# Attention and mixer on one core: k's column maximum sent to all partitions through memory, or by a product with a diagonal

## The chip, the core and the metric

The kernel runs on one core of a Trainium2 chip. The metric is the device time of one execution in microseconds (us). TensorE is called PE here, its weight loads PEld, VectorE DVE, ScalarE ACT, GpSimd POOL and SyncE SP; SP issues the loads. Each engine executes its own instructions in order and waits on semaphores for the others.

## The reference

For 8 batches of 8 heads with 576 positions and 64 channels (all float32), a linear attention is computed and fed to a mixer:

```python
q_s = softmax(q, axis=-1)          # over the 64 channels
k_s = softmax(k, axis=2)           # over the 576 positions
kv  = einsum('bhsd,bhse->bhde', k_s, v)
x   = einsum('bhsd,bhde->bhse', q_s, kv)   # as (batch, 576, 512)
u   = x + w_tok2' relu(w_tok1' x)          # along the positions
out = u + relu(u w_ch1) w_ch2              # along the 512 channels, 1536 hidden
```

The softmax of k subtracts the maximum over all positions for each channel. The mixer's products are held to float32 accuracy by splitting each operand into a high and a low part and adding three products.

## The kernel before, in words

**Units.** A unit is one pair of heads of one batch: 128 channels by 576 positions, padded to 640. There are 32, counted n = 0 to 31. `load_unit` (L106) loads for each unit kt (k with channels on partitions), q, k (positions on partitions; only from unit 8 on) and v. The buffers are few: kt has one, q and k two each, v a ring of two.

**Softmax of k.** `softmax_k` (L179) reduces kt over positions to the maximum mc, one number for each of 128 partitions (L182, DVE). Units 0 to 7 (`on_pe`) take the exponent on kt and turn it with PE. Units 8 to 31 have k with positions on partitions already, so the 128 maxima are wanted along the free axis, on all partitions. The kernel before makes a diagonal matrix dg out of mc (L197, ACT), multiplies a matrix of ones with it on PE (L199), copies the result from PSUM to mb (L201, ACT), subtracts mb from k (L202, POOL) and takes the exponent (L203, ACT).

**The stages of a unit.** After the softmax of q (L211 to L222; its high and low parts are qh, made by ACT, and ql, made by POOL in L89), a unit has four stages: s1 turns q with DVE copies (L262, L270) and multiplies k with v (L229); s2 is the first token product (L281); s3 and s4 are h1 (L289), its split hh and hl (L295, L296), and u (L322), written to the tiles uh and ul (L328, L329).

**The groups.** The positions of all batches are cut into 9 groups of 512. For each group the channel mixer runs 12 steps f: `ch1` (12 matmuls, L341; then h2h by ACT in L343 and h2l by DVE in L344) and, one step later, `ch2` (12 matmuls, L352) into four accumulators ps_o, which `out_end` adds to the residual (L360 by POOL, L367 by DVE) and writes. Units 0 to 3 are computed ahead; in the loop over groups the four units of the next batch are spread between the steps, three steps apart. In the first group the weights are still being loaded and converted on DVE (L143 to L150).

**What sets the order.** The code is written in the order of the loops, but a scheduler, which goes by modelled times, places the instructions of each engine when the program is built (`schedule_with_timeline_sim=True`). So a changed line can move others, and each engine's row of instructions is fixed before the run. One SP queue carries all loads in its row's order; a load that waits for a buffer holds up those behind it.

Of the kernel before, what the change touches and what calls it, by code (L numbers as in the profile page):

```python
# [8 lines left out]
F32 = mybir.dt.float32  # L9
F32R = mybir.dt.float32r  # L10
U32 = mybir.dt.uint32
AF = mybir.ActivationFunctionType
# [3 lines left out]
P = 128  # L16
# [4 lines left out]
def attn_mixer_kernel(ctx: ExitStack, tc: tile.TileContext, q, k, kt, v, wt, out, dims):  # L21
# [3 lines left out]
    nc = tc.nc  # L25
# [14 lines left out]
    const = ctx.enter_context(tc.tile_pool(name="const", bufs=1))  # L40
    ld = ctx.enter_context(tc.tile_pool(name="ld", bufs=2))
    wk = ctx.enter_context(tc.tile_pool(name="wk", bufs=1))
    sm = ctx.enter_context(tc.tile_pool(name="sm", bufs=2))
    stg = ctx.enter_context(tc.tile_pool(name="stg", bufs=2))
    cv = ctx.enter_context(tc.tile_pool(name="cv", bufs=2))
    upool = ctx.enter_context(tc.tile_pool(name="upool", bufs=3))
    hpool = ctx.enter_context(tc.tile_pool(name="hpool", bufs=2))
    ps_o = ctx.enter_context(tc.tile_pool(name="ps_o", bufs=NJ, space=bass.MemoryType.PSUM))
    ps_h = ctx.enter_context(tc.tile_pool(name="ps_h", bufs=4, space=bass.MemoryType.PSUM))

    ident = const.tile([P, P], F32R, name="ident")
# [5 lines left out]
    for t in v_ring:  # L57
        nc.gpsimd.memset(t[:, :, P : P + 1], 1.0)
        nc.gpsimd.memset(t[TL:P, C, :], 0.0)

    ones = const.tile([P, P], F32, name="ones")
    nc.gpsimd.memset(ones, 1.0)


    ebias = const.tile([P, 1], F32, name="ebias")
# [17 lines left out]
    def f32(ap):  # L83
        return ap.bitcast(F32)
# [8 lines left out]
    def ps_unit(dtype=F32):  # L93

        pools = unit_banks[0]
        pool, name = pools[turn[0] % len(pools)]
        turn[0] += 1
        return pool.tile([P, 512], dtype, name=name)
# [80 lines left out]
    def softmax_k(u):  # L179
        ktt = u["kt"]  # L180
        mc = sm.tile([P, 1], F32, name="mc")
        nc.vector.tensor_reduce(mc, ktt, axis=AX.X, op=ALU.max)  # L182
        kx = u["k"]
        if u["on_pe"]:
            nc.vector.tensor_scalar(mc, mc, -1.0, None, op0=ALU.mult)
            nc.scalar.activation(ktt, ktt, AF.Exp, bias=mc)
            t = ps_unit()
            for c in range(C):
                nc.tensor.transpose(t[:, c * P : (c + 1) * P], ktt[:, c * P : (c + 1) * P], f32(ident))
            nc.scalar.copy(kx[:, 0:C, :], t.rearrange("p (c d) -> p c d", c=C))  # L190
            t = ps_unit()
            nc.tensor.transpose(t[:, 0:P], ktt[:, S0 : S0 + P], f32(ident))
            nc.scalar.copy(kx[:, C, :], t[:, 0:P])  # L193
            return

        dg = sm.tile([P, P], F32, name="dg", bufs=1)
        nc.scalar.activation(dg, f32(ident), AF.Copy, scale=mc)  # L197
        t = ps_unit()
        nc.tensor.matmul(t[:, 0:P], ones, dg, start=True, stop=True)  # L199
        mb = sm.tile([P, P], F32, name="mb", bufs=1)  # L200
        nc.scalar.copy(mb, t[:, 0:P])  # L201
        nc.gpsimd.tensor_tensor(kx, kx, mb.unsqueeze(1).broadcast_to([P, C1, P]), op=ALU.subtract)  # L202
        nc.scalar.activation(kx, kx, AF.Exp)  # L203

# [172 lines left out]
    def soft(n):  # L377
        if n < NU:
            softmax_k(units[n])
            softmax_q(units[n])  # L380
# [164 lines left out]
```

## Time and profile before

| | |
|---|---|
| median of 3 runs | 860.49 us (858.84 to 860.98) |
| the profiled execution | 860.69 us, of it 858.6 us span |
| PE, PEld busy | 814.3, 695.5 us |
| DVE, ACT, POOL busy | 494.7, 335.6, 124.4 us |
| moved by DMA | 63.5 MB |

Durations, waits and starts come from the profiled execution alone. Its span is the time from the first to the last instruction; 2.1 us of the execution's own time lie around it. Matmuls are pipelined, so a matmul's listed duration is longer than the time by which it moves the next one on.

### The profile page before, as it was taken

To read this page: it belongs to the slowest core of one execution; us is meant where nothing else is said; L and a number is where in the kernel's file an instruction comes from. 1 tells how busy PE (TensorE), PEld (TensorE's weight loads), DVE (VectorE), ACT (ScalarE), POOL (GpSimd) and SP (SyncE) were. 2 spreads that over 40 slices of the span, in tenths; PEclk is the share of its full clock that TensorE was granted. 3 is DMA by queue.
4 is the path that set the end of the run, shared out by engine and by line. 5 is a ranking of instruction groups with operands and counts; after the bars stand their busy time and mean duration, and the time that the engine had idled before them with its cause. 6 is when DMAs were issued, how large, how long until landed. Compare 5 with 4: busy or idle time off the path is not lost.

```text
span 858.6 us, 11201 instructions
## 1 busy us (share of the span) xinstructions
PE 814.3 (95%) x4224; PEld 695.5 (81%) x4224; DVE 494.7 (58%) x1093; ACT 335.6 (39%) x785; POOL 124.4 (14%) x98
## 2 busy tenths in 40 slices
PE   3668999998999999999999999999999999999997
PEld 2567787877888888888888888888888888888886
DVE  7999998966555755485557555765556332112112
ACT  5676664534434444344444443444434331111100
POOL 0000000422011411041113111311132102001100
PEclk9689999999999999999999999999999999999999
DMA  8435444331112311131122112321121001001001
GB/s 285 133 100 179 146 129 162 94 109 60 60 60 71 99 47 55 37 108 61 60 59 98 59 60 60 110 61 60 45 94 45 1 1 50 1 0 50 1 1 49
DMA packets 41685, 63.50 MB, mean 74 GB/s; under 512 B 3488, under 2 KB 22048, under 8 KB 41632
## 3 DMA queue, kind: packets, MB, share of 16 engines
q1 hardware_dynamic: 36448, 53.36, 19.8%
q10 hardware_dynamic: 5184, 9.44, 2.9%
q8 instruction: 33, 0.54, 0.3%
q14 instruction: 20, 0.16, 0.1%
HBM read 53.35 MB, written 9.44 MB: 73 GB/s over the span
## 4 chain that ended last, share of the span: by engine, by line
PE 79%; DVE 13%; DMA 4%; issue 1%; ACT 1%; POOL 1%; SPq 0%; DVEq 0%; POOLq 0%; ACTq 0%
PE ps_h L341 31%; PE ps_o L352 31%; PE ps_h L322 7%; PE ps_h L281 5%; PE ps_h L229 3%; DMA stg<-in_w 2%; DVE cv_s L145 1%; PE ps_h L289 1%; DVE stg L148 1%; DVE cv_s L150 1%; DVE q_t L270 1%; DMA q_t<-in_q 1%; DVE stg L146 1%; DVE cv_s L143 1%; DVE q_t L212 1%
## 5 line engine op out<-in xcount | busy, mean ns | idle before, releaser
L344 DVE SCALAR_TENSOR_TENSOR h2l<-ps_h,h2h 128x512 fp32r<-128x512 f32 x108 | 74.2, 687 | 182.9 <-ACT h2h L343 182.9
L341 PE MATMUL ps_h<-uh,c1h 128*128 128x512 f32 x432 | 172.6, 400 | 0.9 <-ACT k_t L193 0.7
L341 PE MATMUL ps_h<-ul,c1h 128*128 128x512 f32 x432 | 171.7, 397 | 0.4 <-DVE ul L329 0.4
L341 PE MATMUL ps_h<-uh,c1l 128*128 128x512 f32 x432 | 171.4, 397 | 0.0
L352 PE MATMUL ps_o<-h2h,c2l 128*128 128x512 f32 x432 | 169.0, 391 | 0.0
L343 ACT ACTIVATE h2h<-ps_h 128x512 fp32r<-128x512 f32 x108 | 64.4, 597 | 261.1 <-PE ps_h L341 250.5
L352 PE MATMUL ps_o<-h2h,c2h 128*128 128x512 f32 x432 | 165.1, 393 | 1.5 <-DVE stg L367 1.5
L352 PE MATMUL ps_o<-h2l,c2h 128*128 128x512 f32 x432 | 157.3, 396 | 0.0
L270 DVE COPY q_t<-cv_s 32x160 f32<-32x160 f32 (+1 forms) x264 | 73.3, 278 | 69.9 <-POOL ql L89 66.7
L202 POOL TENSOR_TENSOR k_t<-k_t,mb 128x640 f32<-128x640 f32 x24 | 37.7, 1572 | 459.7 <-ACT mb L201 307.6
L341 PEld LDWEIGHTS ps_h<-ul,c1h 128*128 128x128 f32 x432 | 82.0, 190 | 19.8 <-DVE ul L329 0.6
L341 PEld LDWEIGHTS ps_h<-uh,c1h 128*128 128x128 f32 x432 | 82.2, 190 | 17.5 <-ACT k_t L193 0.9
L352 PEld LDWEIGHTS ps_o<-h2h,c2h 128*128 128x128 f32 x432 | 80.7, 188 | 18.6 <-DVE stg L367 2.6
L341 PEld LDWEIGHTS ps_h<-uh,c1l 128*128 128x128 f32 x432 | 82.2, 190 | 16.5
L352 PEld LDWEIGHTS ps_o<-h2h,c2l 128*128 128x128 f32 x432 | 81.1, 188 | 16.1
L352 PEld LDWEIGHTS ps_o<-h2l,c2h 128*128 128x128 f32 x432 | 79.5, 188 | 15.7
L360 POOL TENSOR_TENSOR stg<-uh,ul 128x512 f32<-128x512 f32 x36 | 47.5, 1343 | 128.4 <-DMA out<-stg 76.6
L211 DVE TENSOR_REDUCE st<-q_t 128x10 f32<-128x640 f32 x32 | 26.2, 819 | 43.8 <-DMA q_t<-in_q 43.8
L89 POOL TENSOR_TENSOR ql<-q_t,qh 128x640 fp32r<-128x640 f32 x24 | 37.9, 1581 | 83.7 <-ACT qh L88 64.1
L229 PEld LDWEIGHTS ps_h<-v_ring,k_t 128*128 128x128 f32 x320 | 44.5, 203 | 4.7 <-ACT qtl L253 2.0
L229 PE MATMUL ps_h<-v_ring,k_t 128*128 128x129 f32 x320 | 46.0, 289 | 1.4 <-ACT qtl L253 1.4
L213 ACT ACTIVATE q_t<-q_t 128x640 f32<-128x640 f32 x32 | 23.7, 740 | 49.7 <-DVE q_t L212 49.7
(136 smaller groups left out, 1223.3 us busy)
## 6 DMA issues: line engine op xcount, KB each, us to landing
stg<-in_w SPq DMA_DIRECT2D x28, 512.0 KB, 3.8
kt_t<-in_kt SPq DMA_DIRECT2D x32, 320.0 KB, 3.2
q_t<-in_q SPq DMA_DIRECT2D x32, 320.0 KB, 2.9
out<-stg ACTq DMA_DIRECT2D x36, 256.0 KB, 2.2
v_ring<-in_v SPq DMA_DIRECT2D x32, 256.0 KB, 2.9
k_t<-in_k SPq DMA_DIRECT2D x24, 320.0 KB, 3.4
v_ring<-in_v SPq DMA_DIRECT2D x32, 32.0 KB, 3.1
stg<-in_w SPq DMA_DIRECT2D x1, 256.0 KB, 6.2
```

What stands on the lines that cost most here:

```text
L89: lo_eng.tensor_tensor(lo, src, f32(hi), op=ALU.subtract)
L202: nc.gpsimd.tensor_tensor(kx, kx, mb.unsqueeze(1).broadcast_to([P, C1, P]), op=ALU.subtract)
L211: nc.vector.tensor_reduce(st[:, 0, :], qt, axis=AX.X, op=ALU.max)
L229: nc.tensor.matmul(kv[:, 0 : P + 1], kx[:, c, :], vt[:, c, 0 : P + 1], start=(c == 0), stop=(c == C))
L270: eng(qx[ys, 0:n, xs], turned[xs, 0:n, ys])
L281: nc.tensor.matmul(y[:, 0:TOK], a, w, start=(i == 0), stop=(i == len(mm) - 1))
L322: nc.tensor.matmul(t[:, 0:N], a, w, start=(i == 0), stop=(i == len(mm) - 1))
L341: nc.tensor.matmul(t, a[:, n, fs], w, start=(i == 0), stop=(i == 3 * NJ - 1))
L343: nc.scalar.activation(hh, t, AF.Relu)
L344: nc.vector.scalar_tensor_tensor(hl, t, 0.0, f32(hh), op0=ALU.max, op1=ALU.subtract)
L352: nc.tensor.matmul(o, a[:, cs], w, start=(f == 0 and i == 0), stop=(f == NF - 1 and i == 2))
L360: nc.gpsimd.tensor_tensor(res[n // 2][:, n % 2, :], f32(uh), f32(ul), op=ALU.add)
```

## The change

For units 8 to 31 the maxima go through memory. One transfer writes mc, a number from each partition, to 512 B of DRAM (`row`); a second reads them back 128 times, so that each partition gets all 128 numbers (mb). The diagonal, the matrix of ones, the product, its PSUM tile and the copy are gone. Subtraction and exponent stay. Both transfers are issued by SP, on the queue of the loads.

```diff
+    dram = ctx.enter_context(tc.tile_pool(name="dram", bufs=2, space=bass.MemoryType.DRAM))
...
-    ones = const.tile([P, P], F32, name="ones")
-    nc.gpsimd.memset(ones, 1.0)
...
-        dg = sm.tile([P, P], F32, name="dg", bufs=1)
-        nc.scalar.activation(dg, f32(ident), AF.Copy, scale=mc)
-        t = ps_unit()
-        nc.tensor.matmul(t[:, 0:P], ones, dg, start=True, stop=True)
+        row = dram.tile([P], F32, name="row")
+        nc.sync.dma_start(row.rearrange("(p x) -> p x", x=1), mc)
         mb = sm.tile([P, P], F32, name="mb", bufs=1)
-        nc.scalar.copy(mb, t[:, 0:P])
+        nc.sync.dma_start(mb, row.unsqueeze(0).broadcast_to([P, P]))
         nc.gpsimd.tensor_tensor(kx, kx, mb.unsqueeze(1).broadcast_to([P, C1, P]), op=ALU.subtract)
         nc.scalar.activation(kx, kx, AF.Exp)
```

The scheduler places much else differently. Lines behind the change have other numbers in the new kernel: the kt, q, k and v loads are L110, L113, L117 and L120 to L121 (L112, L115, L119, L122 to L123 before), the reduction L180 (L182), the subtraction L198 (L202), the copies L266 (L270), h2l L340 (L344), hl L292 (L296), ql L87 (L89). L195 is the row, L197 mb. The number behind a tile's name tells its instance.

SP's loads around units 10 to 13 before; kt_t_2515 and kt_t_2734 are those of units 13 and 14, q_t_2107 is that of unit 11 and q_t_2312 that of unit 12:

```order
L112 DMA kt_t_2515<-in_kt 128x640
L115 DMA q_t_2107<-in_q 128x640
L122 DMA v_ring1_93<-in_v 128x4x128
L119 DMA k_t_2109<-in_k 128x640
L123 DMA v_ring1_93<-in_v 64x128
L112 DMA kt_t_2734<-in_kt 128x640
L115 DMA q_t_2312<-in_q 128x640
```

SP's loads at the same place now, from kt of unit 17 on; mb_2273 is that of unit 11, the rows are those of units 17 to 20, q_t_2101 is q of unit 11:

```order
L110 DMA kt_t_3331<-in_kt 128x640
L197 DMA mb_2273<-row_2271 128x128
L195 DMA row_3507<-mc_3505 128x1
L110 DMA kt_t_3546<-in_kt 128x640
L195 DMA row_3722<-mc_3720 128x1
L110 DMA kt_t_3753<-in_kt 128x640
L195 DMA row_3923<-mc_3921 128x1
L110 DMA kt_t_3954<-in_kt 128x640
L113 DMA q_t_2101<-in_q 128x640
L195 DMA row_4124<-mc_4122 128x1
```

Before, one kt load stood between the loads of two units, two units ahead; now several pairs of row and kt stand there, nine units ahead of q, and between a row and its mb stand the rows of five further units.

DVE around hl of unit 10 before; q_t_2107 is q of unit 11, which is being turned:

```order
L270 COPY q_t_2107<-cv_s_2445 32x5x32 x6
L270 COPY q_t_2107<-cv_s_2445 32x4x32 x5
L296 SCALAR_TENSOR_TENSOR hl_2368<-ps_h_2364,hh_2367 128x256
```

DVE at the same place now; the reductions are those of units 28 to 31:

```order
L180 TENSOR_REDUCE mc_5784<-kt_t_5614 128x1
L340 SCALAR_TENSOR_TENSOR h2l_2311<-ps_h_2312,h2h_2310 128x512
L180 TENSOR_REDUCE mc_5993<-kt_t_5817 128x1
L266 COPY q_t_2101<-cv_s_2437 32x5x32 x6
L266 COPY q_t_2101<-cv_s_2437 32x4x32 x5
L180 TENSOR_REDUCE mc_6210<-kt_t_6034 128x1
L292 SCALAR_TENSOR_TENSOR hl_2360<-ps_h_2356,hh_2359 128x256
L180 TENSOR_REDUCE mc_6413<-kt_t_6243 128x1
```

Reductions of units 28 to 31 now stand between the copies, h2l and hl of unit 10 and 11; the last of all 32 is the one behind hl.

POOL around units 11 and 12 before (k_t_2109 and q_t_2107 are of unit 11, k_t_2314 of unit 12):

```order
L202 TENSOR_TENSOR k_t_2109<-k_t_2109,mb_2281 128x640
L89 TENSOR_TENSOR ql_2294<-q_t_2107,qh_2293 128x640
L202 TENSOR_TENSOR k_t_2314<-k_t_2314,mb_2486 128x640
```

POOL at the same place now (ql_2083 is of unit 10, k_t_2306 of unit 12, q_t_2101 of unit 11):

```order
L87 TENSOR_TENSOR ql_2083<-q_t_1892,qh_2082 128x640
L198 TENSOR_TENSOR k_t_2306<-k_t_2306,mb_2476 128x640
L87 TENSOR_TENSOR ql_2286<-q_t_2101,qh_2285 128x640
```

The subtraction of unit 12 stood behind ql of unit 11 and stands ahead of it now.

## The prediction

> **What bounds the kernel now.** The page's table of engines comes first, then the busy time of each engine in stretches of the span.
>
> ```profile
> PE 814.3 (95%) x4224; PEld 695.5 (81%) x4224; DVE 494.7 (58%) x1093; ACT 335.6 (39%) x785; POOL 124.4 (14%) x98
> ```
> ```profile
> 150.00:175.00 25.00, 24.41 (x132) 21.09 (x132) 24.36 (x46) 12.68 (x31) 9.28 (x6) 1.00 0.27 83
> 175.00:200.00 25.00, 21.35 (x109) 17.47 (x108) 17.11 (x33) 8.92 (x23) 8.13 (x6) 0.99 0.28 94
> 200.00:225.00 25.00, 25.00 (x127) 21.33 (x126) 13.05 (x33) 9.69 (x24) 3.14 (x2) 0.94 0.17 53
> 600.00:680.00 80.00, 80.00 (x432) 69.24 (x431) 42.77 (x102) 32.01 (x81) 15.97 (x11) 1.00 0.15 50
> ```
>
> The columns after a stretch's length are PE, PEld, DVE, ACT, POOL, then the granted clock. From 200 us on PE never rests and DVE is about half idle. From 150 to 175 us DVE is as full as PE, and from 175 to 200 us PE loses 3.65 us. The product that the change removes (L199) first runs at 153.9 us, so nearly all of it lies where PE sets the time.
>
> How much of PE's time one product takes is read from the chain of waits, which follows PE there. A unit is one pair of heads of one batch; units 8 to 31 use this path, 24 in all, and the product for unit n stands right behind L229 of unit n-1.
>
> ```profile
> 153.88 0.22 PE ps_h L199 x2
> ...
> 250.97 0.22 PE ps_h L199 x2
> ...
> 677.69 0.22 PE ps_h L199 x2
> ```
> ```profile
> L199 PE MATMUL ps_h<-dg,ones x48: 272/274/275, 153.7 to 677.6; 128*128 128x128 f32 x48
> ```
>
> The first, the fifth and the last of the 24 are shown: each moves the chain on by 0.22 us, although its two passes are listed with 274 ns each, because matmuls overlap. The 0.22 is the price; 24 times two times 0.274 (13.2 us) would count the overlap.
>
> **The change, part by part.** What it removes from PE is 24 x 0.22 = 5.3 us, four of them (units 8 to 11) before 245 us and 20 (4.4 us) after it. From ACT it removes two operations for each unit:
>
> ```profile
> L197 ACT ACTIVATE dg<-ident,mc x24: 402/405/417, 136.8 to 656.0; 128x128 f32<-128x128 f32 x24
> L201 ACT COPY mb<-ps_h x24: 245/248/265, 154.2 to 677.9; 128x128 f32<-128x128 f32 x24
> ```
>
> That is 24 x (0.405 + 0.248) = 15.7 us of an engine that is busy 39%; PE's work covers it, so I count nothing.
>
> What it adds are 48 small transfers on SP's queue, a write of 512 B (row) and a read of 64 KB (mb) for each unit. How long such a pair takes is bounded by the nearest transfers: the output, which goes to memory, and v's tail, which is read.
>
> ```profile
> out<-stg ACTq DMA_DIRECT2D x36, 256.0 KB, 2.2
> v_ring<-in_v SPq DMA_DIRECT2D x32, 32.0 KB, 3.1
> ```
>
> 2.2 + 3.1 = 5.3 us from maximum to subtraction. Only units 8 and 9 can feel this. For unit 8 the reduction and the next q load stand so:
>
> ```profile
> 135.33 0.81 DVE L182 TENSOR_REDUCE mc<-kt_t 128x1 f32<-128x640 f32 x1
> ```
> ```profile
> 140.64 0.33 SPq L115 DMA_DIRECT2D q_t<-in_q  x1
> ```
>
> The row lands at 135.33 + 0.81 + 0.33 + 2.2 = 138.7 us, so SP, which waits for it before it issues mb, is free again 1.9 us before q of unit 9 goes out anyway. If that cover were gone, it would cost its 2.2 us twice at most.
>
> From unit 10 on the rows run far ahead, and here lies what the order does besides. The reduction's result no longer waits for an ACT operation and a PE product of its own unit, so kt loads and reductions of units 10 to 31 are pulled forward: in the new order the last reduction stands just behind L296 of unit 10, while the old order has one in each unit. These are linked. There is one kt buffer: the load of unit n+1 waits for the reduction of unit n, and on SP it stands behind the row of unit n. DVE executes in order, so a reduction whose kt has not landed holds up everything behind it. One link costs:
>
> ```profile
> L112 SPq DMA_DIRECT2D kt_t<-in_kt x32: 327/333/549, 0.7 to 590.2; - x32
> ...
> DMA to landing us min/median/max: 2.8/3.2/6.6
> ```
> ```profile
> L182 DVE TENSOR_REDUCE mc<-kt_t x32: 799/809/829, 4.0 to 611.8; 128x1 f32<-128x640 f32 x32
> ```
>
> The reduction is 0.81, the row's issue (as that of kt) 0.33, and kt's landing 2.8 to 3.2: 3.95 to 4.35 us, plus what the row's own packets cost the kt load that follows them in the same queue. I take 4.3: the landing at 3.15, since k, v and q loads still fall among these.
>
> What is available? The relevant rows of DVE and PE:
>
> ```profile
> 186.45 1.25 DVE L367 TENSOR_TENSOR stg<-ps_o,stg 128x512 f32<-128x512 f32 x2
> ...
> 193.01 4.80 DVE L270 COPY q_t<-cv_s 32x160 f32<-32x160 f32 x11 [4.72 <-POOL ql L89]
> 197.84 0.43 DVE L296 SCALAR_TENSOR_TENSOR hl<-ps_h,hh 128x256 fp32r<-128x256 f32 x1
> ```
> ```profile
> 241.42 0.42 DVE L296 SCALAR_TENSOR_TENSOR hl<-ps_h,hh 128x256 fp32r<-128x256 f32 x1 [1.15 <-ACT hh L295]
> ```
> ```profile
> 244.91 0.31 PE L322 MATMUL ps_h<-w2h,hl 128*128 128x320 f32 x1
> ```
>
> The reduction of unit 17 stands behind the four L367 of the first group, which end at 187.70 us. The reduction of unit 30 stands right ahead of L296 of unit 10, whose result PE takes at 244.91 us; it must therefore end by 244.91 - 0.42 = 244.49. That leaves (244.49 - 187.70) / 13 = 4.37 us for each of 13 links, and one link is longer anyway, because DVE has the eleven copies and L296 in it: 4.80 + 0.43 + 0.81 = 6.04, which is 1.74 over 4.3. With 4.3 the sum is 187.70 + 13 x 4.3 + 1.74 = 245.34, L296 ends at 245.76, and PE gets its input 0.85 us later than now. Whatever PE gained before that (four products, and the wait treated next) is used up there. Behind it DVE has no such reductions left, about half of its time is free, and the 20 products count in full.
>
> The gain before it, if the links allow it, has a second part. At the first change of groups PE waits for DVE to empty the accumulators, and a reduction stands among those operations:
>
> ```profile
> 184.30 0.50 PE L352 MATMUL ps_o<-h2h,c2h 128*128 128x512 f32 x1 [0.56 <-DVE stg L367]
> 185.63 0.51 PE L352 MATMUL ps_o<-h2h,c2h 128*128 128x512 f32 x1 [0.36 <-DVE stg L367]
> 187.16 0.50 PE L352 MATMUL ps_o<-h2h,c2h 128*128 128x512 f32 x1 [0.56 <-DVE stg L367]
> ```
>
> At most 0.56 + 0.36 + 0.56 = 1.48 us; at least nothing, since q's softmax stands there too.
>
> POOL changes places as well: k's subtraction of unit n+1 now stands ahead of ql of unit n, where it stood behind it. So ql waits for k's load:
>
> ```profile
> k_t<-in_k SPq DMA_DIRECT2D x24, 320.0 KB, 3.4
> ```
> ```profile
> 228.78 0.46 SPq L119 DMA_DIRECT2D k_t<-in_k  x1
> ```
> ```profile
> 235.94 1.56 POOL L89 TENSOR_TENSOR ql<-q_t,qh 128x640 fp32r<-128x640 f32 x1 [4.95 <-ACT qh L88]
> ```
> ```profile
> 255.81 1.67 PE ps_h L281 x14
> ```
>
> k lands at 228.78 + 3.4 = 232.2; a subtraction as long as ql's 1.56 ends at 233.7, and ql starts at 235.94 today: 2.2 us to spare. If they were gone, ql would be late, but the product that reads it runs at 255.81, so I count nothing. In the steady part mb stands ahead of the next unit's q load on SP and waits for the subtraction before, which is over by then.
>
> The sum: 860.69 us is the profiled execution's own time (858.6 span), 0.20 above the median of 860.49. 860.69 + 0.85 - 4.4 = 857.1 us.
>
> **The rivals.** First, the links don't bite: at 3.95 us they are done long before 244.49, and PE keeps all: 24 x 0.22 + 1.48 = 6.8 us, so 853.9. For it speaks that the lower landing is 2.8; against it, that k, v and q loads stand among the links.
>
> Second, on the other side, the row's packets hold up the kt load behind them. A row is 128 pieces of 4 B from 128 partitions, eight for each of 16 engines, and the queue's mean packet costs
>
> ```profile
> q1 hardware_dynamic: 36448, 53.36, 19.8%
> ```
>
> 0.198 x 16 x 858.6 / 36448 = 75 ns. Eight of them take 0.6 us, the link becomes 4.9, the sum 187.70 + 63.7 + 1.14 + 0.42 = 252.96, PE is 8.05 us late there and 860.69 + 8.05 - 4.4 = 864.3. Against it: these pieces are far smaller than the mean (53.36 MB over 36448 packets, 1464 B). It decides from a link of about 4.8 us on, where the loss passes the gain by 0.3%. The Trainium skill's page "DMA: Bandwidth & Descriptors", section "Specifications", states that the DMA engine reads, modifies and writes what is under 512 B; an estimate that doubles the packet for it has 1.2 us and a link of 5.5, and 871.5 us. No row of this profile shows such a write, so it is part of this rival, not its centre.
>
> Third, the change does not free what the chain says. Behind the product the next L352 starts only 0.14 us after it:
>
> ```profile
> 250.81 0.39 PE L199 MATMUL ps_h<-dg,ones 128*128 128x128 f32 x2
> 250.95 0.71 PE L352 MATMUL ps_o<-h2l,c2h 128*128 128x512 f32 x2
> ```
>
> If only 0.14 is freed, 20 x 0.14 = 2.8, and 860.69 + 0.85 - 2.8 = 858.7 us, no difference. Against it stands that three steps of the chain agree on 0.22.
>
> **How the numbers follow.** The forecast has a chance of 0.5, the first rival 0.2, the second 0.2, the third 0.1. The forecast's own range, links of 4.05 to 4.55, is 12 x 0.25 = 3.0 us to either side (the long link does not depend on it): 854.1 to 860.1. A measurement tells about 0.3% from no change, 2.6 us, so faster means under 857.9 and slower over 863.1. The forecast lies under 857.9 in 0.6 of its cases (0.3) and else between; with the first rival faster has 0.5, with the third no difference 0.2 + 0.1 = 0.3, and the second is slower, 0.2. The range goes from just under the first rival (853.5) to the second's time (864.3); the rest of the second's cases lies beyond.
>
> **What would show it.** Right: L199, L197 and L201 are gone; a unit in the steady part (300 to 680 us) takes 0.22 us less; reductions come every 4.3 us or so from 188 to 245 us, with DVE waiting for kt before some of them; L296 of unit 10 ends near 246 us, and PE waits before L322 there and hardly anywhere later. Wrong: no DVE waits for kt (first rival); links of 4.8 us or more and PE waits of several us up to 260 us (second); a steady unit as long as before (third); or PE waiting for kx or ql in the steady part, for which I count nothing.

## The result, and the profile after

The changed kernel takes 1017.04 us (median of 6 runs, 1015.49 to 1020.38) against 859.64 us of the kernel before (6 runs, 858.55 to 860.98). The ratio is 1.1837, 95% interval 1.1824 to 1.185: slower by 157 us. The profiled execution has a span of 1013.5 us.

The page of the changed kernel, its PE and the clock granted to PE in 40 slices of 25 us:

```profile
PE 849.8 (84%) x4176; PEld 717.6 (71%) x4176; DVE 496.1 (49%) x1093; ACT 323.9 (32%) x737; POOL 124.7 (12%) x97
...
PE   3779977555752544899999999999999999999997
...
PEclk9989997967677776999999999999999999999999
```

The loss has a place. From the eighth to the sixteenth slice (about 175 to 400 us) PE is busy 20 to 60% of the time in all slices but the eleventh (7 tenths); behind them PE is full, as before. It begins a little earlier, soon after the first row (135.2 us). In numbers, by stretches (PE busy, its count, the granted clock, DMA share, GB/s):

```profile
150.00:175.00 25.00, 18.32 (x77) 0.80 0.52 99
175.00:200.00 25.00, 15.19 (x66) 0.93 0.54 27
200.00:225.00 25.00, 11.34 (x46) 0.67 0.57 42
...
500.00:600.00 100.00, 100.00 (x532) 1.00 0.18 56
```

The stretch from 200 to 225 us, which had 25.00 us of PE and 53 GB/s at a DMA share of 0.17, now has 11.34 us, and the DMA engines are busy three times as much (0.57) to move less (42 GB/s). That is the first hint: something holds the DMA engines that moves nearly nothing. The granted clock falls to 0.67 here, where PE rests more than half of the time, and a matmul is listed as longer in such stretches: the first product with hl (128x320) with 0.64 us at 318.33, with 0.31 at 244.91 in the kernel before. So PE's busy sum is larger than before (849.8 against 814.3 us) though there is less work.

DVE's waits name what is late (us in all, times, the longest), and the page's list of transfers how long it takes from issue to landing, the last figure of each line:

```profile
DVE mc L180 <- DMA kt_t<-in_kt: 136.4, 20, 11.2
```
```profile
kt_t<-in_kt SPq DMA_DIRECT2D x32, 320.0 KB, 10.1
...
mb<-row SPq DMA_DIRECT2D x24, 64.0 KB, 2.9
```

A kt load landed in 3.2 us before and lands in 10.1 now, though it moves the same 320 KB. In front of most of the 32 stands a row:

```profile
L195 SPq DMA_DIRECT2D row<-mc x24: 319/326/383, 135.2 to 401.9; - x24
...
DMA to landing us min/median/max: 7.3/7.9/9.9
```

512 B take 7.9 us to land, and the last of 24 rows goes out at 401.9 us, just where PE's loss ends. The read of 64 KB behind it (mb) lands in 2.9 us. One link of the chain of kt, reduction and row, on SP, then on DVE, and what PE then waits for:

```profile
306.19 0.32 SPq L195 DMA_DIRECT2D row<-mc  x1
306.61 0.38 SPq L110 DMA_DIRECT2D kt_t<-in_kt  x1
317.97 0.32 SPq L195 DMA_DIRECT2D row<-mc  x1
```
```profile
305.35 0.82 DVE L180 TENSOR_REDUCE mc<-kt_t 128x1 f32<-128x640 f32 x1 [10.21 <-DMA kt_t<-in_kt]
...
317.12 0.82 DVE L180 TENSOR_REDUCE mc<-kt_t 128x1 f32<-128x640 f32 x1 [8.32 <-DMA kt_t<-in_kt]
317.86 0.41 DVE L292 SCALAR_TENSOR_TENSOR hl<-ps_h,hh 128x256 fp32r<-128x256 f32 x1
...
389.31 0.82 DVE L180 TENSOR_REDUCE mc<-kt_t 128x1 f32<-128x640 f32 x1 [8.74 <-issue]
390.04 0.41 DVE L292 SCALAR_TENSOR_TENSOR hl<-ps_h,hh 128x256 fp32r<-128x256 f32 x1
```
```profile
318.33 0.64 PE L318 MATMUL ps_h<-w2h,hl 128*128 128x320 f32 x1 [14.64 <-DVE hl L292]
...
390.51 0.63 PE L318 MATMUL ps_h<-w2h,hl 128*128 128x320 f32 x1 [17.41 <-DVE hl L292]
```

In the last reduction shown, `issue` stands for a wait whose end the profile puts down to nothing. A reduction ends and the row goes out (306.19), then kt (306.61); the next reduction starts 10.51 us after that, and DVE stood still in front of it for 8.32 us. hl, which PE wants, stands behind that reduction, and PE waits 14.64 us for it. 23 links lie between the first row (135.2) and the last (401.9): 11.6 us each.

The gain is there too. The chain of waits, before and after, at the same 24 matmuls of successive units in the steady part (L352 before is L348 now):

```profile
504.70 5.47 PE ps_o L352 x24
...
572.01 5.47 PE ps_o L352 x24
```
```profile
504.37 5.47 PE ps_o L348 x24
...
570.99 5.47 PE ps_o L348 x24
```

Three units took 67.31 us and take 66.62: 22.44 and 22.21 us each, 0.23 less.

### The profile page after: what moved, and what is told of

Its sections match the earlier page's. It is cut to its first block, busy times and chain, and to the rows that moved or that the text cites. A ratio compares the mean times of both kernels' runs of the same rounds, so it can differ in the third digit from the quotient of the medians.

```text
span 1013.5 us, 11178 instructions
## 1 busy us (share of the span) xinstructions
PE 849.8 (84%) x4176; PEld 717.6 (71%) x4176; DVE 496.1 (49%) x1093; ACT 323.9 (32%) x737; POOL 124.7 (12%) x97
## 4 chain that ended last, share of the span: by engine, by line
PE 56%; DVE 2%; DMA 1%; issue 1%; POOL 0%; ACT 0%; DVEq 0%; POOLq 0%; SPq 0%; ACTq 0%
PE ps_o L348 23%; PE ps_h L337 23%; PE ps_h L318 5%; PE ps_h L277 3%; PE ps_h L225 2%; DMA q_t<-in_q 1%; PE ps_h L285 1%; DVE q_t L266 0%; DMA out<-stg 0%; POOL stg L356 0%; DVE h2l L340 0%; DVE stg L363 0%; DVE st L207 0%; DVE q_t L208 0%; POOL ql L87 0%
## 5 line engine op out<-in xcount | busy, mean ns | idle before, releaser
L348 PE MATMUL ps_o<-h2h,c2h 128*128 128x512 f32 x432 | 170.9, 407 | 19.3 <-ACT h2h L339 14.1
L348 PE MATMUL ps_o<-h2h,c2l 128*128 128x512 f32 x432 | 174.5, 404 | 6.2 <-DVE c2l L87 6.2
L348 PE MATMUL ps_o<-h2l,c2h 128*128 128x512 f32 x432 | 161.1, 413 | 19.8 <-DVE h2l L340 15.4
L340 DVE SCALAR_TENSOR_TENSOR h2l<-ps_h,h2h 128x512 fp32r<-128x512 f32 x108 | 74.0, 685 | 195.0 <-ACT h2h L339 194.9
L198 POOL TENSOR_TENSOR k_t<-k_t,mb 128x640 f32<-128x640 f32 x24 | 37.8, 1576 | 655.0 <-DMA k_t<-in_k 346.1
L348 PEld LDWEIGHTS ps_o<-h2h,c2h 128*128 128x128 f32 x432 | 84.4, 197 | 38.1 <-ACT h2h L339 15.3
L180 DVE TENSOR_REDUCE mc<-kt_t 128x1 f32<-128x640 f32 x32 | 26.1, 817 | 173.8 <-DMA kt_t<-in_kt 136.4
L348 PEld LDWEIGHTS ps_o<-h2l,c2h 128*128 128x128 f32 x432 | 83.0, 197 | 38.6 <-DVE h2l L340 22.3
L348 PEld LDWEIGHTS ps_o<-h2h,c2l 128*128 128x128 f32 x432 | 84.6, 196 | 24.0 <-DVE c2l L87 6.9
L266 DVE COPY q_t<-cv_s 32x160 f32<-32x160 f32 (+1 forms) x264 | 69.6, 264 | 38.5 <-POOL ql L87 35.2
L318 PE MATMUL ps_h<-w2h,hl 128*128 128x256 f32 (+1 forms) x120 | 33.8, 321 | 39.6 <-DVE hl L292 39.6
L225 PE MATMUL ps_h<-v_ring,k_t 128*128 128x129 f32 x320 | 51.1, 310 | 14.1 <-DVE h2l L340 12.7
L225 PEld LDWEIGHTS ps_h<-v_ring,k_t 128*128 128x128 f32 x320 | 48.7, 221 | 18.5 <-DVE h2l L340 14.0
L324 ACT CAST uh<-ps_h 128x320 fp32r<-128x320 f32 (+4 forms) x84 | 26.4, 331 | 86.6 <-DVE ul L325 51.2
## 6 DMA issues: line engine op xcount, KB each, us to landing
kt_t<-in_kt SPq DMA_DIRECT2D x32, 320.0 KB, 10.1
```

The source lines that it names most:

```text
L225: nc.tensor.matmul(kv[:, 0 : P + 1], kx[:, c, :], vt[:, c, 0 : P + 1], start=(c == 0), stop=(c == C))
L266: eng(qx[ys, 0:n, xs], turned[xs, 0:n, ys])
L318: nc.tensor.matmul(t[:, 0:N], a, w, start=(i == 0), stop=(i == len(mm) - 1))
L324: nc.scalar.copy(uh, src)
L340: nc.vector.scalar_tensor_tensor(hl, t, 0.0, f32(hh), op0=ALU.max, op1=ALU.subtract)
L348: nc.tensor.matmul(o, a[:, cs], w, start=(f == 0 and i == 0), stop=(f == NF - 1 and i == 2))
```

## The experiments

The runs began with three theories. W: the row's slow write lengthens each link to 11.7 us, and DVE stands still at the reductions placed ahead. R: the round trip of row and mb for each unit is what costs. P: reductions placed ahead cost, whatever the link. "Before" was timed beside every kernel: 859.8, 860.09, 859.34 and 860.26 us in the four sets (the 11 runs below come in this order).

**1. The write taken away.** mb is read from 128 of k's own numbers, so another number than the maximum is subtracted, and mb no longer waits for a row; reductions stay far ahead.

```diff
-        row = dram.tile([P], F32, name="row")
-        nc.sync.dma_start(row.rearrange("(p x) -> p x", x=1), mc)
...
-        nc.sync.dma_start(mb, row.unsqueeze(0).broadcast_to([P, P]))
+        nc.sync.dma_start(mb, k[u["n"]][0:1, 0:P].broadcast_to([P, P]))
```

> The changed kernel without the row's write; mb is read from 128 numbers of in_k, so the maximum that is subtracted is not k's. Reductions still run far ahead. W: kt lands in about 3.2 us again, a link is about 4.3, and the time is what the prediction said of such links, 857 us, 853 to 862. Theory P (reductions placed ahead on DVE cost by their place, whatever the link): still over 950 us. R: also fast, since the round trip is gone.

861.22 us (9 runs), ratio to before 1.0024 (1.0009 to 1.0038). 156 of the 157 us are gone with the write. DVE's rows show a chain like the one that the prediction worked out, without the row (L264, L290 and L316 are here the copies, hl and u's product with it):

```profile
186.89 0.81 DVE L180 TENSOR_REDUCE mc<-kt_t 128x1 f32<-128x640 f32 x1
...
244.79 0.82 DVE L180 TENSOR_REDUCE mc<-kt_t 128x1 f32<-128x640 f32 x1 [2.47 <-DMA kt_t<-in_kt]
245.53 2.72 DVE L264 COPY q_t<-cv_s 32x160 f32<-32x160 f32 x11
248.28 0.43 DVE L290 SCALAR_TENSOR_TENSOR hl<-ps_h,hh 128x256 fp32r<-128x256 f32 x1
```
```profile
200.69 0.64 PE L316 MATMUL ps_h<-w2h,hl 128*128 128x320 f32 x1 [4.33 <-DVE hl L290]
```

Between the two reductions shown, those of units 18 and 31, are 13 links (4.45 us each), and hl of unit 10 behind them ends at 248.71 us. PE waits only 0.31 us for that one. It waits longer for hl of unit 8 (the last line, 4.33 us; 2.17 in the kernel before), which stands behind the reductions of units 19 and 20; DVE waited 1.98 us for kt in front of the first of them. So reductions ahead are not what costs 157 us: P fails as an account of it.

**2. The run-ahead held.** A small GpSimd instruction behind the subtraction reads mc. Since mc has two buffers, a reduction can be at most two units ahead. The computation is complete.

```diff
+        held = sm.tile([P, 1], F32, name="held")
+        nc.gpsimd.tensor_tensor(held, mc, kx[:, 0, 0:1], op=ALU.add)
```

> The changed kernel, with one small operation on POOL behind k's subtraction that reads mc, so that a maximum's buffer is free only then and reductions can run ahead by two units at most, as before the change; both transfers stay. Theory W (the row's write lands in 7.3 to 9.9 us, the kt load behind it in 10.1, and DVE stands still at reductions that were placed ahead): a reduction then has a whole unit of 22 us for its link of 11.7, nothing waits for it, and PE keeps 24 x 0.22 = 5.3 us: 855 us, 853 to 858. Theory R (what costs is the round trip of row and mb, 7.9 + 2.9 us for each unit): the trip is as long as in the changed kernel and nearer to its use, so well over 900 us.

879.06 us (6 runs, 871.61 to 885.51); the ratio, without the longest of them, is 1.0201 (1.017 to 1.0231). R fails: the same 24 round trips are there, and most of the loss is gone. But W misses too, by 24 us. The chain of waits of this kernel has the row in it at several places:

```profile
134.42 10.14 DMA row<-mc
144.58 3.29 DMA mb<-row
...
161.06 8.17 DMA k_t<-in_k
...
472.97 7.27 DMA row<-mc
```

SP stands at mb until the row has landed (134.42 to 144.58), and k's load, issued at 161.06, lands in 8.17 us where 3.4 is its median. Whether it is SP's standing or a hold on other transfers is left to the runs 10 and 11.

**3. The row on another queue.** ACT issues the write, so that nothing of SP's stands behind it in its queue.

```diff
-        nc.sync.dma_start(row.rearrange("(p x) -> p x", x=1), mc)
+        nc.scalar.dma_start(row.rearrange("(p x) -> p x", x=1), mc)
```

> The changed kernel with the row's write issued by ACT instead of SP, so that it is in another queue than the kt load. W, if it is the queue that makes kt wait: kt lands in about 3.2 us, 857 to 870 us. W, if the write holds the DMA engines or the memory themselves: kt lands in about 10 us still, and the time stays near 1015 us. R: near 1015 us too, since the row lands as late.

1000.82 us (2 runs), ratio 1.1641 (1.1613 to 1.1669). The landing of the kt loads, on a queue that now holds no row:

```profile
L110 SPq DMA_DIRECT2D kt_t<-in_kt x32: 327/328/531, 0.7 to 369.5; - x32
...
DMA to landing us min/median/max: 2.8/9.0/12.7
```

9.0 us: the order within SP's queue is not what delays kt. The write delays transfers of another queue. The Trainium skill, page "DMA: Bandwidth & Descriptors", section "Issuing engines are not separate DMA queues", says that transfers run on the same 16 DMA engines whichever engine starts them; the 9.0 us of kt beside a row of another queue agree with it.

**4. Four forms of the write.** Nothing reads them, and mb comes from k's own numbers as in run 1. Each unit writes in one of four forms in turn: side by side as the changed kernel does, 4 B every 64 B, 4 B every 512 B, and 128 pieces of 512 B.

```diff
+        form = u["n"] % 4
+        if form == 0:
             row = dram.tile([P], F32, name="row")
             nc.sync.dma_start(row.rearrange("(p x) -> p x", x=1), mc)
+        elif form == 1:
+            far = dram.tile([P, 16], F32, name="far")
+            nc.sync.dma_start(far[:, 0:1], mc)
+        elif form == 2:
+            farther = dram.tile([P, P], F32, name="farther")
+            nc.sync.dma_start(farther[:, 0:1], mc)
+        else:
+            full = dram.tile([P, P], F32, name="full")
+            nc.sync.dma_start(full, u["kt"][:, 0:P])
```

> As the run without the row's write (mb from in_k, so another maximum is subtracted), with a write that nobody reads in one of four forms by unit: 128 pieces of 4 B side by side, as in the change; 4 B every 64 B; 4 B every 512 B; 128 pieces of 512 B (128 columns of kt). If small pieces are slow by themselves, the first three land in about 8 us and the fourth in about 3. If pieces that lie in one stretch of 512 B stand in each other's way, only the first takes 8, the second less, and the third about 3.

One run, 906.64 us. The landings of the first form, the second and the last:

```profile
L197 SPq DMA_DIRECT2D row<-mc x6: 326/326/330, 136.0 to 278.1; - x6
...
DMA to landing us min/median/max: 7.7/8.3/9.9
```
```profile
L200 SPq DMA_DIRECT2D far<-mc x6: 326/326/327, 147.9 to 287.5; - x6
...
DMA to landing us min/median/max: 1.4/1.4/2.2
```
```profile
L206 SPq DMA_DIRECT2D full<-kt_t x6: 326/326/327, 157.1 to 295.3; - x6
...
DMA to landing us min/median/max: 1.5/1.5/1.6
```

128 pieces of 4 B take 8.3 us side by side and 1.4 us with 64 B from one to the next (1.4 at 512 B too). 128 times as many bytes in the same number of pieces take 1.5 us. So neither the count of the pieces nor their smallness is slow, but small pieces that lie close together.

**5. How close.** Six forms in turn; again nothing reads them.

```diff
+        if form == 0:
+            pitch8 = dram.tile([P, 2], F32, name="pitch8")
+            nc.sync.dma_start(pitch8[:, 0:1], mc)
...
+        elif form == 3:
+            clump = dram.tile([8, P], F32, name="clump")
+            nc.sync.dma_start(clump[:, 0:16].unsqueeze(2), mc)
+        elif form == 4:
+            inner = sm.tile([1, P], F32, name="inner")
+            nc.sync.dma_start(inner, mc)
```

> Nothing reads these writes, and the maximum that is subtracted is another one (128 of k's own numbers), so only times are read. Each unit from 8 to 31 writes its 128 maxima in one of six forms: 4 bytes every 8, every 16, every 32 bytes, in eight clumps of 16 pieces side by side (64 bytes) that stand 512 bytes apart, into 512 bytes of one SBUF partition, and side by side in memory as the changed kernel does. Known so far: side by side 8.3 us, every 64 bytes 1.4 us. Theory L (pieces that share 64 bytes of memory are written one after the other, (8.3 - 1.4) / 15 = 0.46 us each): 4.6, 2.8 and 1.9 us for 8, 16 and 32 bytes, 8.3 us for the clumps. Theory S (pieces that share 512 bytes wait for one another, 6.9 / 127 = 0.054 us each): 4.8, 3.1 and 2.2 us, and 2.2 us for the clumps. Both: SBUF is no memory of that kind, so 1.4 to 2 us there; a theory by which small pieces side by side are slow wherever they go says 8 us there too. The whole run lies between 861 and 960 us, by how many of the forms are slow.

One run, 909.92 us. Every 8 B (L197):

```profile
L197 SPq DMA_DIRECT2D pitch<-mc x4: 326/326/326, 165.1 to 294.5; - x4
...
DMA to landing us min/median/max: 3.6/3.7/3.7
```

Side by side takes 8.1 us, every 8 B 3.7, every 16 B and every 32 B 1.4, one SBUF partition 1.9. Neither theory's line fits: both wanted 2.8 us or more at 16 B. A write's own landing does not tell all, though. The kt load behind it landed in 7.7, 11.3 and 10.6 us behind the side-by-side form, in 5.9 and 5.8 at 8 B, in 4.4 and 4.5 at 16 B, and in 3.3 at 32 B, where 3.2 is its time in the kernel before. So at 16 B the write lands in 1.4 us and still costs the load behind it more than 1 us. The clumps' landing is not in the trace; the two kt loads behind them whose landing it has took 4.8 and 4.9 us, where L wanted some 10 and S some 3. The rule by which close pieces hold each other up stays open. That SBUF is not touched by it is what the next run uses.

**6. The row by way of SBUF.** The maxima go into one partition, from there to memory in one piece of 512 B. The computation is complete, and reductions run far ahead.

```diff
-        row = dram.tile([P], F32, name="row")
-        nc.sync.dma_start(row.rearrange("(p x) -> p x", x=1), mc)
+        inner = sm.tile([1, P], F32, name="inner")
+        nc.sync.dma_start(inner, mc)
+        row = dram.tile([1, P], F32, name="row")
+        nc.sync.dma_start(row, inner)
...
-        nc.sync.dma_start(mb, row.unsqueeze(0).broadcast_to([P, P]))
+        nc.sync.dma_start(mb, row.broadcast_to([P, P]))
```

> The maxima go into one SBUF partition first (128 pieces of 4 bytes), from there to memory in one piece of 512 bytes, and mb is read from that as before: the full computation, with reductions still placed far ahead. W (only the row's slow write to memory counts; the link without it is 4.3 us, since the new row write stands behind the next kt load on SP): 860 us, 857 to 864, inner landing in 1.4 to 2 us and kt in 3. A theory by which 128 small pieces hold up the loads behind them wherever they are written: links of 10 us or more again, over 960 us. A theory by which a round trip through memory for each unit is what costs (three transfers now, not two): over 1020 us.

863.13 us (4 runs), ratio 1.0042 (1.0026 to 1.0058), in W's range. Three transfers for each unit in place of two, and 154 us less than the changed kernel. The landings are not in this trace.

**7. The same with the hold.**

```diff
+        held = sm.tile([P, 1], F32, name="held")
+        nc.gpsimd.tensor_tensor(held, mc, kx[:, 0, 0:1], op=ALU.add)
```

> The last with the hold on the run-ahead (a GpSimd instruction that reads mc behind the subtraction, so a reduction is at most two units ahead). If what was left of 20 us with the hold alone came from the slow write (SP standing 8 to 10 us at mb with the loads of q, k and v behind it, kt landing in 10.6): 856 us, 854 to 859, faster than before by 0.1 to 0.6 per cent. If it came from the hold itself (DVE and GpSimd waiting for each other): near 879 us still.

855.21 us (6 runs, 853.95 to 857.34), ratio 0.9948 (0.9934 to 0.9963): with the whole computation 0.5% faster than the kernel before. The 24 us that run 2 missed were the slow write's and not the hold's, since these two differ in the way of the row alone. Its page and its first transfer:

```profile
PE 807.9 (95%) x4176; PEld 686.4 (80%) x4176; DVE 494.4 (58%) x1093; ACT 325.7 (38%) x737; POOL 133.7 (16%) x121
...
kt_t<-in_kt SPq DMA_DIRECT2D x32, 320.0 KB, 3.2
```
```profile
L195 SPq DMA_DIRECT2D inner<-mc x24: 481/483/536, 134.7 to 611.7; - x24
...
DMA to landing us min/median/max: 1.9/1.9/2.0
```

PE is busy for 807.9 us in place of 814.3, and kt lands in 3.2 us as before the change.

**8. The hold without any write.** Run 1 with the hold; another number is subtracted there too.

```diff
         nc.sync.dma_start(mb, k[u["n"]][0:1, 0:P].broadcast_to([P, P]))
...
+        held = sm.tile([P, 1], F32, name="held")
+        nc.gpsimd.tensor_tensor(held, mc, kx[:, 0, 0:1], op=ALU.add)
```

> No write at all, mb read from k's own numbers (another maximum is subtracted), and the hold on the run-ahead. This is what the change would be with a write that costs nothing and no links: the gain of 0.22 us on PE for each of 20 to 24 units alone, 855 us (854 to 857). If the links of 4.3 us were not what took back the gain in the run without the write (861.2 us), it stays at 861.

854.52 us (5 runs), ratio 0.9936 (0.9924 to 0.9948), 5.6 us under before. That is the gain by itself, and it fits 24 products of 0.22 to 0.23 us (5.3 to 5.5). Run 1, with its run-ahead, stands 6.7 us higher, and the traces show where: from 125 to 300 us PE runs 858 matmuls there and 899 here, from 300 to 690 us 2063 in both. PE's waits for hl, 5.0 us of that stretch in run 1, are not among its waits here.

**9. The run-ahead alone, in the kernel before.**

```diff
-        mc = sm.tile([P, 1], F32, name="mc")
+        mc = sm.tile([P, 1], F32, name="mc", bufs=24)
```

> The kernel before with its product of ones and diagonal, and 24 buffers for mc in place of 2, so that the reductions are placed as far ahead as in the changed kernel and follow one another by the one kt buffer, with no row and no mb. If the run-ahead alone takes what the run without the write lost against the one that was held (861.2 - 854.5 = 6.7 us), it comes to 864 to 870 us. If reductions ahead cost nothing by themselves (and it is the mb transfers on SP that took it), it stays at 860. A theory by which the run-ahead, not the write, makes most of the 157 us: over 900.

859.81 us (10 runs), ratio 1.0011 (0.9997 to 1.0026). The reductions do follow one another every 3.6 to 4.2 us from 200 to 239 us, and no loss can be measured. But this chain is faster than the forecast's 4.3 us and run 1's 4.45: its last reduction ahead of hl of unit 10 ends at 239.62 us, and hl (244.87) waits for ACT's hh and not for a reduction. So run 9 shows that links of up to 4.2 us cost nothing; P falls for these and for the 157 us. For the 6.7 us of run 1 it stays open how far the longer links, the mb transfers on SP, or the places of the copies share in them.

**10. The slow row beside the kernel before.** Product path and order of before, and a row for each unit that nothing reads.

```diff
+    dram = ctx.enter_context(tc.tile_pool(name="dram", bufs=2, space=bass.MemoryType.DRAM))
...
+        row = dram.tile([P], F32, name="row")
+        nc.sync.dma_start(row.rearrange("(p x) -> p x", x=1), mc)
```

> The kernel before, with its product path and its order of one reduction to each unit, and the slow row written beside it (128 pieces of 4 bytes side by side, once per unit), which nothing reads. kt should land in 10 us again, as it stands behind the row on SP. W (the write costs where a chain or SP's queue waits for it, and nowhere else: here kt has a whole unit of 22 us): 861 us, 859 to 864. A theory by which the write costs by holding the engines and the memory for all transfers (row 8 us by 24 units is 192 us of them): 870 to 890 us.

909.1 us (4 runs), ratio 1.0582 (1.0545 to 1.062). W's 861 is far off, and the loss is even above the rival's 870 to 890: nobody waits for this row, and it costs 50 us. The chain of waits says how:

```profile
134.38 10.32 DMA kt_t<-in_kt
...
163.23 16.41 DMA stg<-in_w
...
210.28 10.65 DMA out<-stg
```

A weight load takes 16.41 us (3.9 is the median), and an output write, which ACT issues on its own queue, 10.65 (median 2.4). Most of the loss lies between 130 and 250 us, where the weights still come in and the groups change. That stretch in this run, then in the kernel before (PE busy, its count, the granted clock, DMA share, GB/s):

```profile
130.00:250.00 120.00, 90.48 (x429) 0.87 0.45 68
```
```profile
130.00:250.00 120.00, 114.32 (x597) 0.99 0.27 87
```

PE runs 429 matmuls there in place of 597, at a granted clock of 0.87. In the steady part most of the delay finds slack.

**11. The same with 64 B between the pieces.**

```diff
-        row = dram.tile([P], F32, name="row")
-        nc.sync.dma_start(row.rearrange("(p x) -> p x", x=1), mc)
+        far = dram.tile([P, 16], F32, name="far")
+        nc.sync.dma_start(far[:, 0:1], mc)
```

> The last run but one again (the kernel before, with a write of the 128 maxima per unit beside it that nothing reads), with the 128 pieces of 4 bytes every 64 bytes in place of side by side. If the 49 us that the unread row cost came from its pieces' lying side by side (they hold up every transfer behind and beside them): 860 us, 859 to 862, kt landing in 3 us and far in 1.4. If one more write of 128 small pieces for each unit on SP's queue, or the order that it makes, is what cost: 900 to 910 us again.

862.15 us (10 runs, 859.74 to 866.18), ratio 1.0024 (1.0007 to 1.004). The page's transfers:

```profile
kt_t<-in_kt SPq DMA_DIRECT2D x32, 320.0 KB, 3.2
...
far<-mc SPq DMA_DIRECT2D x24, 0.5 KB, 1.6
```

The same pieces on the same queue, with SP's loads and writes in the same order, cost 2 us in place of 50. So the place of the pieces in memory is the cause of the 50 us.

## Why the prediction was wrong

It said 857.1 us (853.5 to 864.3), and the kernel takes 1017.04. By its steps:

**PE's gain held.** 0.22 us for each product was forecast, 0.23 is measured, and the two runs without the slow write and with the hold stand 4.9 and 5.6 us under before.

**ACT's 15.7 us** were counted at nothing, and no run speaks against it: PE's term of 5.3 us makes up the gain of run 8 but for 0.3 us.

**The failed step is the price of the row's write**, and in the sum of a link the term "what the row's own packets cost the kt load that follows them in the same queue". The forecast's 4.3 us put that term at nothing without a row for it; the second rival gave it 0.6 us, eight packets of 75 ns. The runs showed 6.9 us: the kt load lands in 10.1 us behind a row and in 3.2 without (an estimate from these: 0.86 us for each of eight packets, over ten times the mean one). The row itself was bounded by the output's landing of 2.2 us and lands in 7.9. The rows used as bounds were of pieces of 2 KB (the output) and 512 B (v's tail); the kernel before has no row of small pieces written side by side, and the bounds left that open on the upper side. The same price broke the cover of unit 8: SP got past its mb at 144.35 us and issued q of unit 9 at 144.77, in place of 140.64.

**The links were right in mechanism, wrong in size.** One kt buffer, kt behind the row on SP, DVE held up at the reductions, PE waiting for hl of unit 10 in front of its L318: all of it is in the trace. The link was put at 4.3 us. Thirteen links plus the long one's extra were to take 57.6 us; without the slow write (run 1) thirteen took 57.9. That agreement is in part luck: run 1's order is another, its links are those from unit 18 to 31 and not 17 to 30, no row is issued in them (0.33 us each), and the eleven copies (2.72 us) stand behind the last reduction. hl of unit 10 ended there at 248.71 in place of the forecast 245.76, and the main wait came at hl of unit 8, which the sum left out; run 1 takes 861.22 us, 4 more than the forecast, and run 6, with its reductions ahead too, 863.13. So even with a fast write the forecast's sum was low by 4 to 6 us for reductions placed ahead. With the write a link is 11.8 us. The chain was to start at 187.70 us, and the reduction of unit 17 starts at 235.86, 48.2 us late already; 13 links to 389.31 take 153.5 us in place of 57.6, and hl of unit 10 ends at 390.45, 144.7 us late. That is most of the 160 us that were missed; behind it PE loses another 5.4 us from 400 to 450 us, while q's loads catch up, and the rest was not followed.

**The handover of the accumulators, POOL's order and the steady part.** For POOL's changed order nothing was counted, and the steady unit's 22.21 us leaves no room for a cost. The handover's wait of 1.48 us can't be judged in the changed kernel, where the stretch is late for another reason; for the accumulators PE waits 1.3 us in run 8 and 1.2 in run 7, and not at all in run 1, where it waits 0.40 us for h2l at that place. So the forecast's bounds, nothing to 1.48 us, hold.

**The rivals.** The second one named the mechanism (the row's packets hold up the kt load behind) and the point from which it decides (a link of 4.8 us), and priced it at 0.6 us; it is 6.9. Its estimate by the size rule of the Trainium skill, page "DMA: Bandwidth & Descriptors", section "Specifications" (less than 512 B is read, modified and written), gave 871.5. The runs don't follow a rule by size alone: 4 B at 64 B distance are below 512 B too and land in 1.4 us. The first rival (853.9, links that don't bite) comes near run 7's 855.2, but for another reason: there the reductions are held, and no chain of links exists. The third fails by the steady unit.

**W, the theory of the first runs, fell in part.** It had the write cost only where a chain or SP's queue waits for it. The unread row costs 50 us, and the delayed output write on ACT's queue shows that the write holds up transfers of both queues in use. The run-ahead alone costs at most 2.2 us in the kernel before (ratio 1.0026 at the upper end), and 6.7 us in the change without its write; the write with the run-ahead held costs 19 us (run 2). The two together cost 157, because the chain of one kt buffer waits for each delayed transfer in turn.

## What to carry to other kernels

A transfer's bytes say little: ask how its pieces lie where they are written. One number from each of 128 partitions, side by side in memory, took 8 us and slowed the transfers under way beside it; gathered in one SBUF partition first (1.9 us) and written in one piece, it was harmless, and with the run-ahead held the change then gained 0.5%. Where a scheduler may pull a step far ahead, one single-buffered load becomes a chain, and the price of each link is paid once for every unit placed ahead.

## What the runs showed of the hardware

- 128 writes of 4 B from 128 partitions, issued by SP, land in 7.9 to 8.3 us side by side (medians of five kernels), in 3.7 us from 8 B to 8 B, and in 1.4 us from 16, 32, 64 or 512 B to the next (1.6 in run 11). A 320 KB load behind such a write lands in 10.1 us with the pieces side by side, and in 5.8 to 5.9, 4.4 to 4.5 and 3.3 us from 8, 16 and 32 B to the next.
- Transfers under way beside the side-by-side write are slow on the other queue too: kt 9.0 us with the row on ACT's queue, an output write 10.65 us on ACT's with the row on SP's.
- The same 128 pieces into one SBUF partition land in 1.9 us, and the loads behind them aren't delayed in the median (kt 3.2 us, run 7).
- PE's granted clock was 0.59 to 0.80 in the stretches from 200 to 400 us in which PE rested a third of the time or more.
